# Column stage of an FFT mixer: the turn of U in three pieces, conversion slots moved, one product tile in PSUM

## The chip, the core and the metric

One core of a Trainium2 chip runs the whole program. The metric is device microseconds (us) of one execution; less is better. TensorE (PE) multiplies, VectorE (DVE), ScalarE (ACT) and GpSimd (POOL) work on tiles, and SyncE (SP) issues most DMAs. PEld is TensorE's weight load. All engines run their own queue strictly in order and wait for each other through semaphores.

## What is computed

```python
X = np.fft.rfft(x, axis=1)                       # x: 4 x 3136 x 256
y = np.fft.irfft(X * (filt_r + 1j * filt_i), n=3136, axis=1)
h = y.transpose(0, 2, 1) @ U @ V                 # U: 3136 x 32, V: 32 x 3136
u = y + h.transpose(0, 2, 1)
u = u + np.maximum(u @ w_ch1, 0.0) @ w_ch2       # 256 -> 1024 -> 256
xn = (u - mean) / np.sqrt(var + 1e-06) * g_ln    # over the 256 channels
out = u + np.maximum(xn @ w_ch1b, 0.0) @ w_ch2b
```

U, V and the weights arrive as 64-bit floats.

## The kernel before

The Fourier transform along the 3136 tokens is made by matmuls with tables, as 112 x 28. The program records all instructions in a fixed order; each engine's queue is that order, filtered by engine. It has three parts.

The first batch's transform runs alone. `rows()` turns 7 blocks of x by the row tables. Then `columns()` handles 14 pairs of 28 groups in 17 steps, j = 0 to 16; it is the stage of the change, and what follows names its parts as the text does later:
- **psz(j)**, L653: TensorE transposes pair 13 - j out of `big` into PSUM, ScalarE copies it to SBUF (z0). Odd steps take the PSUM pool ps_h (tag h, three banks), even ones ps_t (tag t, one bank).
- **ps2(j)**, L667: the pair of the step before is turned by the table e; then `filtered` multiplies it by the filter on VectorE: two products straight from PSUM (ya L635, xs L639) and two half sums (L641, L642), which GpSimd makes, or VectorE for the last pair (i = 0, step 14, with the products L638). ps2 takes banks of ps_h.
- **ps3(j)**, L678, from step 3 on: the pair that went through ps2 two steps earlier is multiplied back by the table d, whose last 32 columns hold the turned U, into two of the four output banks (`outer`, tags o0 to o3, in rotation). In the step after, ScalarE copies the result back into `big` (the spill) and VectorE adds the 32 columns of each bank to a sum (L622, L624), each behind the spill of the same bank.
- the **turn** of U, `u_half(1)` and then `u_half(0)`: a transposition on VectorE (L557), then one or two matmuls (pst, L562 and L563), the scaled copies uf by VectorE (L566) and the four copies uq by ScalarE (L219). From step 2 on, ScalarE copies a slice of uq into the table slot (`d<-uq`) of the pair that needs it two steps later.
- the filter loads for step j + 3 on SP's queue, and in step 1 two copies on GpSimd (L685) that fill the table slots.
- the **conversion slots**: `next(pr)` takes the conversion of weights and V from 64-bit to 32-bit numbers one slot further. A conversion begins every four slots: two reads by ScalarE (L976, L977), four operations on VectorE (L963, L965, L967, L969, one a slot), a product (L981) and a sum (L983) on GpSimd, three slots after the sum a copy by ScalarE (w1h, w2h, vh) and a slot later the low half on GpSimd (L1054, L1099). `COLSLOTS` says in which steps the slots lie: as often as it names a step, so many slots has it.

`UTURN` lists the steps in which the turn goes on by one piece; `UTURN.index(j) // 2` picks the half. In step 11 GpSimd issues the load of V (v_sb). Then `mixed` and `part` turn the columns back into tokens (psw, L725), and the first units (psu, L783, L785) begin.

The second part, most of the time, is the two-layer blocks, with the other three batches' transforms between them; the third is the rest of the blocks. `outer` gives them banks too.

Of the kernel before, what the change touches and what calls it, by code (L numbers as in the profile page):

```python
# [10 lines left out]
F32 = mybir.dt.float32  # L11
# [22 lines left out]
WARM, KEEP = 11, (0, 10, 5, 2, 2, 4, 1)  # L34
PUS, UTURN = ((), (0, 1), (2,), (3,), (4,), (5,), (6,)), (0, 1, 2, 3)
BACKL = 3
# [5 lines left out]
ROWSLOTS = (1, 2, 2, 3, 4, 5, 5, 5, 6)  # L42
COLSLOTS = (0, 0, 1, 1, 2, 2, 3, 3) + tuple(range(4, 12))
VSTEP = 11
# [139 lines left out]
def fft_mixer_kernel(ctx: ExitStack, tc: tile.TileContext, x, U, V, flt, w1, w2, gln, w1b, w2b,  # L184
# [261 lines left out]
    class First:  # L446
# [103 lines left out]
        def u_half(self, h):  # L550
# [13 lines left out]
            for lo, hi, wc in ((14, 28, w_sb[:, 0:1]),) if h else ((0, 1, w_sb[:, 1:2]), (1, 14, w_sb[:, 0:1])):  # L564
                src = ps[:, (lo - 14 * h) * R:(hi - 14 * h) * R].rearrange("p (g r) -> p g r", r=R)
                nc.vector.tensor_scalar(out=self.uf[:, lo:hi], in0=src, scalar1=wc, scalar2=None, op0=ALU.mult)  # L566
            for g in range(2):
                for k in range(2):
# [33 lines left out]
        def columns(self):  # L602
# [23 lines left out]
            def filtered(i, ps):  # L626
# [3 lines left out]
                else:  # L630
                    xs = fp.tile([P, 2, D], F32, tag="xs", name="xs", bufs=2)
                    ya = fp.tile([P, 2, D], F32, tag="ya", name="ya", bufs=4)
                src = ps.rearrange("p (a d) -> p a d", a=2)
                if i:
                    nc.vector.tensor_tensor(out=ya, in0=src, in1=f[:, 0:1].to_broadcast([P, 2, D]), op=ALU.mult)  # L635
                else:
                    for k, fr in enumerate((f[:, 0], self.nyquist)):
                        nc.vector.tensor_tensor(out=ya[:, k], in0=src[:, k], in1=fr, op=ALU.mult)  # L638
                nc.vector.tensor_tensor(out=xs, in0=src, in1=f[:, 1:2].to_broadcast([P, 2, D]), op=ALU.mult)  # L639
                eng = nc.gpsimd if i else nc.vector  # L640
                eng.tensor_tensor(out=ya[:, 0], in0=ya[:, 0], in1=xs[:, 1], op=ALU.subtract)  # L641
                eng.tensor_tensor(out=ya[:, 1], in0=ya[:, 1], in1=xs[:, 0], op=ALU.add)  # L642
                ys[i] = ya

            due = None
            for j in range(n + BACKL):
# [33 lines left out]
                if j in UTURN:  # L680
                    next(turns[UTURN.index(j) // 2], None)
                self.filters(j + AHEAD)
# [24 lines left out]
        def part(self, u, between=None):  # L707
# [4 lines left out]
            for dh in range(KT):  # L712
# [7 lines left out]
                if u < 2:  # L720
                    ps = outer("psw")
                else:
                    ps = (ps_t if dh else ps_h).tile([P, 512], F32, tag="t" if dh else "h", name="psw")
# [540 lines left out]
```

## Time and profile before

| | before |
|---|---|
| three timed runs | 1341.11, 1348.93, 1348.85 us; median 1348.85 |
| the profiled execution | 1340.96 us |
| its span in the profile | 1339.2 us |
| mean granted TensorE clock, share of full speed | 0.996 |
| TensorE busy | 1309.8 us (98%) |
| VectorE busy | 803.5 us (60%) |
| ScalarE busy | 428.9 us (32%) |
| GpSimd busy | 151.7 us (11%) |

Times in rows are us from the span's start. Busy shares are averages over stages with different limits, so the rows below are taken from the column stage. The row of a timeline gives start, duration (of several operations together, if it ends in a count over 1), engine, line, operation and its tiles; in brackets the engine's idle time ahead of it and what ended that.

### The profile page before, as it was taken

The page shows a single profiled execution, that of the slowest core. Times are in us where ns is not written, and L with a number is a line of the kernel's source. Part 1 is how long each engine was busy: PE and PEld are TensorE (multiplying, and loading weights), DVE is VectorE, ACT ScalarE, POOL GpSimd, SP SyncE. Part 2 cuts the span into 40 slices and gives each one's busy share as a digit, 9 for nine tenths or more (in the row PEclk, how much of TensorE's full clock was granted, in tenths as well). Part 3 has the DMA queues.
Part 4 walks back from the last instruction along what each step waited for, and adds up shares of the span by engine and source line. Part 5 has one row for each costly group of instructions (what it writes and reads, how often), then busy time and mean ns, then how long its engine had stood idle before and what let it go on. Part 6 is the DMA issues. An engine that isn't in the chain of part 4 may idle for free.

```text
span 1339.2 us, 22454 instructions
## 1 busy us (share of the span) xinstructions
PE 1309.8 (98%) x8606; PEld 1045.3 (78%) x8606; DVE 803.5 (60%) x1643; ACT 428.9 (32%) x857; POOL 151.7 (11%) x133
## 2 busy tenths in 40 slices
PE   8899999999999999999999999999999999999998
PEld 7578677777777877877777777878888888888887
DVE  5676985666656566575655666565455545555454
ACT  4456542333332233233322232232222222222222
POOL 1745530112000010010000010100000000000000
PEclk9899999999999999999999999999999999999999
DMA  9634447576565455434543554532112202210111
GB/s 236 173 99 140 114 109 220 150 226 173 148 178 148 120 150 145 127 99 114 165 144 96 140 159 113 144 90 65 32 34 65 65 16 67 65 40 9 47 49 40
DMA packets 166531, 151.15 MB, mean 113 GB/s; under 512 B 65912, under 2 KB 142568, under 8 KB 166424
## 3 DMA queue, kind: packets, MB, share of 16 engines
q1 hardware_dynamic: 166120, 148.25, 40.3%
q0 software_dynamic: 304, 1.47, 0.5%
q8 instruction: 68, 1.11, 0.3%
q14 instruction: 39, 0.32, 0.1%
HBM read 91.10 MB, written 47.54 MB: 104 GB/s over the span
## 4 chain that ended last, share of the span: by engine, by line
PE 85%; DVE 6%; DMA 4%; ACT 2%; SPq 2%; issue 1%; POOL 1%; DVEq 0%; POOLq 0%; ACTq 0%
PE psh L821 37%; PE pso L848 13%; PE pso L849 6%; PE pso L840 6%; PE pso L841 6%; PE pso L842 6%; PE psu L798 2%; DMA x<-x 2%; PE ps L301 1%; PE ps L375 1%; PE ps L341 1%; PE ps L678 1%; PE psu L803 1%; DVE hl L825 1%; PE ps L667 1%
## 5 line engine op out<-in xcount | busy, mean ns | idle before, releaser
L825 DVE SCALAR_TENSOR_TENSOR hl<-psh,hh 128x512 fp32r<-128x512 f32 (+1 forms) x400 | 271.5, 680 | 359.5 <-ACT hh L824 358.1
L824 ACT ACTIVATE hh<-psh 128x512 fp32r<-128x512 f32 (+1 forms) x400 | 234.8, 588 | 657.8 <-PE psh L821 657.6
L848 PE MATMUL pso<-wb,hh 128*128 128x512 f32 x784 | 285.0, 397 | 0.5 <-DVE x2t L888 0.3
L821 PE MATMUL psh<-ah,wb 128*128 128x512 f32 (+1 forms) x800 | 281.1, 393 | 0.6 <-DVE hl L825 0.6
L849 PE MATMUL pso<-wb,hl 128*128 128x256 f32 x784 | 219.7, 280 | 0.0
L821 PEld LDWEIGHTS psh<-ah,wb 128*128 128x128 f32 x800 | 150.1, 188 | 47.0 <-issue 6.0
L848 PEld LDWEIGHTS pso<-wb,hh 128*128 128x128 f32 x784 | 147.6, 188 | 35.4 <-DVE x L863 0.8
L821 PE MATMUL psh<-ah,w1h 128*128 128x512 f32 (+1 forms) x400 | 158.1, 395 | 0.0
L841 PE MATMUL pso<-hl,w2h 128*128 128x512 f32 (+1 forms) x400 | 154.4, 386 | 2.8 <-DVE hl L825 2.8
L840 PE MATMUL pso<-hh,w2h 128*128 128x512 f32 (+1 forms) x400 | 155.9, 390 | 0.4 <-DVE x2t L888 0.3
L821 PE MATMUL psh<-al,wb 128*128 128x512 f32 (+1 forms) x400 | 155.9, 390 | 0.0
L821 PE MATMUL psh<-al,w1h 128*128 128x512 f32 (+1 forms) x400 | 155.2, 388 | 0.0
L821 PE MATMUL psh<-ah,w1l 128*128 128x512 f32 (+1 forms) x400 | 154.3, 386 | 0.0
L842 PE MATMUL pso<-hh,w2l 128*128 128x512 f32 (+1 forms) x400 | 154.0, 385 | 0.0
L849 PEld LDWEIGHTS pso<-wb,hl 128*128 128x128 f32 x784 | 148.2, 189 | 7.5
L357 POOL TENSOR_TENSOR xs<-xs,ft 128x512 f32<-128x512 f32 x42 | 57.0, 1357 | 650.3 <-ACT hh L824 241.0
L821 PEld LDWEIGHTS psh<-ah,w1h 128*128 128x128 f32 x400 | 75.1, 188 | 22.5 <-issue 3.9
L888 DVE SCALAR_TENSOR_TENSOR x2t<-pso,ln,x2t 128x256 f32<-128x256 f32 x196 | 89.7, 480 | 3.6
L840 PEld LDWEIGHTS pso<-hh,w2h 128*128 128x128 f32 x400 | 75.1, 188 | 20.8 <-issue 5.6
L841 PEld LDWEIGHTS pso<-hl,w2h 128*128 128x128 f32 x400 | 75.2, 188 | 18.2 <-DVE hl L825 3.9
L821 PEld LDWEIGHTS psh<-ah,w1l 128*128 128x128 f32 x400 | 75.2, 188 | 15.9
L842 PEld LDWEIGHTS pso<-hh,w2l 128*128 128x128 f32 x400 | 75.1, 188 | 15.1
(150 smaller groups left out, 1341.7 us busy)
## 6 DMA issues: line engine op xcount, KB each, us to landing
ft<-flt SPq DMA_DIRECT2D x42, 512.0 KB
xd<-x SPq DMA_DIRECT2D x96, 128.0 KB
x2t<-xd SPq DMA_DIRECT2D x24, 512.0 KB
wt<-bd SPq DMA_DIRECT2D x48, 224.0 KB
out<-x2t SPq DMA_DIRECT2D x84, 128.0 KB
xs<-zc SPq DMA_DIRECT2D x168, 64.0 KB
xt<-x SPq DMA_DIRECT2D x84, 112.0 KB
zd<-ze SPq DMA_DIRECT2D x84, 112.0 KB
```

The costliest lines, as they stand in the source:

```text
L301: nc.tensor.matmul(pss[j][quarter(h), m * D:(m + 1) * D], ct[rows56(j), 2 * h + m], xs[h][rows56(j), m], start=True, stop=True)
L357: nc.gpsimd.tensor_tensor(out=xs, in0=xs, in1=fi[:, e], op=ALU.mult)
L798: nc.tensor.matmul(pss[h][c * HALF:(c + 1) * HALF, dh, h * spare + m:h * spare + half:UW], t[rows, m, d0:d0 + HALF], ic[rows, m, :], start ...
L821: nc.tensor.matmul(ps[:, :n], w[:, kt, fs], a[:, kt, :n], start=j == 0, stop=j == 3 * KT - 1)
L824: nc.scalar.activation(out=hh[:, :n], in_=ps[:, :n], func=AF.Relu)
L825: nc.vector.scalar_tensor_tensor(out=hl[:, :n], in0=ps[:, :n], scalar=0.0, in1=f32(hh[:, :n]), op0=ALU.max, op1=ALU.subtract)
L840: nc.tensor.matmul(o, wh[:, f, ds], hh[:, :n], start=f == 0, stop=False)
L841: nc.tensor.matmul(o, wh[:, f, ds], hl[:, :n], start=False, stop=False)
L842: nc.tensor.matmul(o, wl[:, f, ds], hh[:, :n], start=False, stop=f == FT - 1)
L848: nc.tensor.matmul(o, hh[:, cs], w, start=f == 0, stop=False, skip_group_check=True)
L849: nc.tensor.matmul(o[:, D:], hl[:, cs], w[:, :D], start=False, stop=f == FT - 1, skip_group_check=True)
L888: nc.vector.scalar_tensor_tensor(out=o, in0=acc[c][:, half * D:(half + 1) * D], scalar=rs[:, c:c + 1], in1=o, op0=ALU.mult, op1=ALU.add)
```

## The change

The turn of a half now has three pieces: the transposition, then the matmuls with uf, and, behind a new `yield`, the four uq copies. `UTURN` puts the pieces of the first half into steps 0, 1 and 2, those of the second into 3, 4 and 6 (before: two pieces each in steps 0 to 3). `COLSLOTS` gives one conversion slot each to steps 0 to 3, two to steps 4 to 7 and one to 8 to 11 (before: two in 0 to 3, one in 4 to 11); there are 16 both times. For the last pair the two products with the filter's real part go to a tile `yr` in PSUM (pool ps_t), from which the two sums are made. And the psw of part 0 takes banks of ps_h in place of output banks, so every output bank from there on is two further round the four.

```diff
-PUS, UTURN = ((), (0, 1), (2,), (3,), (4,), (5,), (6,)), (0, 1, 2, 3)
+PUS, UTURN = ((), (0, 1), (2,), (3,), (4,), (5,), (6,)), (0, 1, 2, 3, 4, 6)
...
-COLSLOTS = (0, 0, 1, 1, 2, 2, 3, 3) + tuple(range(4, 12))
+COLSLOTS = (0, 1, 2, 3) + tuple(j // 2 for j in range(8, 16)) + tuple(range(8, 12))
...
                 nc.vector.tensor_scalar(out=self.uf[:, lo:hi], in0=src, scalar1=wc, scalar2=None, op0=ALU.mult)
+            yield
             for g in range(2):
...
+                yr = ya
                 if i:
                     nc.vector.tensor_tensor(out=ya, in0=src, in1=f[:, 0:1].to_broadcast([P, 2, D]), op=ALU.mult)
                 else:
+                    yr = ps_t.tile([P, 512], F32, tag="t", name="yr").rearrange("p (a d) -> p a d", a=2)
                     for k, fr in enumerate((f[:, 0], self.nyquist)):
-                        nc.vector.tensor_tensor(out=ya[:, k], in0=src[:, k], in1=fr, op=ALU.mult)
+                        nc.vector.tensor_tensor(out=yr[:, k], in0=src[:, k], in1=fr, op=ALU.mult)
                 nc.vector.tensor_tensor(out=xs, in0=src, in1=f[:, 1:2].to_broadcast([P, 2, D]), op=ALU.mult)
                 eng = nc.gpsimd if i else nc.vector
-                eng.tensor_tensor(out=ya[:, 0], in0=ya[:, 0], in1=xs[:, 1], op=ALU.subtract)
-                eng.tensor_tensor(out=ya[:, 1], in0=ya[:, 1], in1=xs[:, 0], op=ALU.add)
+                eng.tensor_tensor(out=ya[:, 0], in0=yr[:, 0], in1=xs[:, 1], op=ALU.subtract)
+                eng.tensor_tensor(out=ya[:, 1], in0=yr[:, 1], in1=xs[:, 0], op=ALU.add)
...
                 if j in UTURN:
-                    next(turns[UTURN.index(j) // 2], None)
+                    next(turns[UTURN.index(j) // 3], None)
...
                 if u < 2:
-                    ps = outer("psw")
+                    ps = outer("psw") if u else inner("psw")
```

The line numbers below are those of each kernel's own source: from L567 on they are one higher after the change, from L634 on two, from L637 on three.

ScalarE's queue, steps 1 to 4, before (z_435 and z_479 are psz of steps 1 and 2, z_505 of step 3):

```order
L219 ACTIVATE z_435<-psz 112x512
L219 ACTIVATE uq<-uf 64x224 x4
L219 ACTIVATE w1h<-ct 128x512
L976 ACTIVATE cyh<-stg 128x392
L977 ACTIVATE cyl<-stg 128x392
L219 ACTIVATE z_479<-psz 112x512
L219 ACTIVATE d_187<-uq 128x2x32 x2
L219 ACTIVATE z_505<-psz 112x512
L219 ACTIVATE uq<-uf 64x224 x4
```

The same place after the change (z_434, z_463, z_488 and z_534 are steps 1 to 4):

```order
L219 ACTIVATE z_434<-psz 112x512
L219 ACTIVATE z_463<-psz 112x512
L219 ACTIVATE uq<-uf 64x224 x4
L219 ACTIVATE d_187<-uq 128x2x32 x2
L219 ACTIVATE z_488<-psz 112x512
L219 ACTIVATE d_187<-uq 128x2x32
L219 ACTIVATE w1h<-ct 128x512
L979 ACTIVATE cyh<-stg 128x392
L980 ACTIVATE cyl<-stg 128x392
L219 ACTIVATE z_534<-psz 112x512
```

Step 2's copy has moved ahead of the first uq copies and of the conversion, which now stands behind step 3's copy; the second uq copies have left the place altogether.

VectorE's queue, steps 4 and 5, before (ps_518 and ps_519 are ps3 of step 3, ps_578 and ps_579 of step 4):

```order
L622 COPY d_188<-ps_518 128x2x32
L622 COPY d_188<-ps_519 128x2x32
L635 TENSOR_TENSOR ya<-ps_567,f_301 128x512
L639 TENSOR_TENSOR xs<-ps_567,f_301 128x512
L963 TENSOR_SCALAR cyh<-cyh 128x512
L624 TENSOR_TENSOR d_188<-ps_578,d_188 128x2x32
L624 TENSOR_TENSOR d_188<-ps_579,d_188 128x2x32
```

The same place after the change (ps_501 and ps_502, ps_551 and ps_552):

```order
L623 COPY d_188<-ps_501 128x2x32
L623 COPY d_188<-ps_502 128x2x32
L637 TENSOR_TENSOR ya<-ps_540,f_301 128x512
L642 TENSOR_TENSOR xs<-ps_540,f_301 128x512
L566 TENSOR_SCALAR uf<-pst,w_sb 128x32
L566 TENSOR_SCALAR uf<-pst,w_sb 128x416
L966 TENSOR_SCALAR cyh<-cyh 128x392
L968 TENSOR_SCALAR ct<-cyh 128x392
L625 TENSOR_TENSOR d_188<-ps_551,d_188 128x2x32
L625 TENSOR_TENSOR d_188<-ps_552,d_188 128x2x32
```

Between step 4's products and the sums of its banks there are now four operations where there was one: uf of the second half and two of a conversion.

VectorE's queue, steps 14 and 15, after the change; before, the first two rows and the two sums have ya for yr, and the rest is the same:

```order
L641 TENSOR_TENSOR yr<-ps_949,f_788 128x256
L641 TENSOR_TENSOR yr<-ps_949,f_828 128x256
L642 TENSOR_TENSOR xs<-ps_949,f_788 128x512
L644 TENSOR_TENSOR ya<-yr,xs 128x256
L645 TENSOR_TENSOR ya<-yr,xs 128x256
L625 TENSOR_TENSOR d_188<-ps_962,d_188 128x2x32
L625 TENSOR_TENSOR d_188<-ps_963,d_188 128x2x32
```

No operation has moved here; what has changed is the memory in which the tile between them lies.

On TensorE only the second half's pst has moved, from behind step 3's ps3 to behind step 4's. On GpSimd the filter sums of steps 2 and 3 now stand ahead of a conversion's product (L981). On SP's queue one group of filter loads has moved ahead of two staging loads.

## Rows read from the trace of the kernel before

**Rows 1.** Windows: length; busy us by engine (instructions); granted clock; DMA share; GB/s.
```profile
38.00:48.40 10.40, 5.31 (x44) 3.38 (x44) 5.94 (x13) 6.77 (x19) 7.37 (x9) 1.00 0.75 205
48.40:55.50 7.10, 7.10 (x43) 5.20 (x43) 3.68 (x9) 1.23 (x4) 3.91 (x5) 0.52 0.85 207
55.50:78.00 22.50, 22.50 (x228) 15.71 (x228) 16.60 (x38) 13.19 (x39) 17.51 (x21) 1.00 0.54 142
...
140.00:180.00 40.00, 36.17 (x154) 25.79 (x154) 39.47 (x55) 18.72 (x35) 23.64 (x17) 1.00 0.42 108
```

**Rows 2.** Timeline of TensorE, step 10 and the start of step 11.
```profile
66.62 0.65 PE L653 MATMUL psz<-ident,big 128*112 128x128 f32 x4
67.20 1.08 PE L667 MATMUL ps<-z,e 112*64 112x256 f32 x8
68.21 1.26 PE L678 MATMUL ps<-d,ya 64*128 64x144 f32 x16
69.40 0.65 PE L653 MATMUL psz<-ident,big 128*112 128x128 f32 x4
```

**Rows 3.** Timeline of all engines, steps 2 and 3.
```profile
34.45 0.60 PE L653 MATMUL psz<-ident,big 128*112 128x128 f32 x4
...
35.93 1.59 ACT L219 ACTIVATE uq<-uf 64x224 f32<-64x224 f32 x4 [2.91 <-DVE uf L566]
...
37.13 1.00 POOL L685 COPY d<-d 128x336 f32<-128x336 f32 x2
...
38.98 0.57 ACT L219 ACTIVATE z<-psz 112x512 f32<-112x512 f32 x1
...
39.61 1.08 PE L667 MATMUL ps<-z,e 112*64 112x256 f32 x8 [2.96 <-ACT z L219]
```

**Rows 4.** Timeline of all engines, the second half's turn and step 4.
```profile
43.04 0.81 DVE L566 TENSOR_SCALAR uf<-pst,w_sb 128x32 f32<-128x32 f32 x2 [1.01 <-PE pst L563]
...
43.88 1.59 ACT L219 ACTIVATE uq<-uf 64x224 f32<-64x224 f32 x4 [3.55 <-DVE uf L566]
...
48.38 2.25 PE L678 MATMUL ps<-d,ya 64*128 64x144 f32 x14 [3.48 <-DVE d L622]
```

**Rows 5.** Timeline of all engines, steps 14 to 16.
```profile
78.88 0.76 DVE L638 TENSOR_TENSOR ya<-ps,f 128x256 f32<-128x256 f32 x2 [0.17 <-PE ps L667]
...
79.94 1.29 POOL L1054 TENSOR_TENSOR w2l<-ct,w2h 128x512 fp32r<-128x512 f32 x1
...
80.27 1.25 DVE L641 TENSOR_TENSOR ya<-ya,xs 128x256 f32<-128x256 f32 x1
...
81.44 1.48 DVE L642 TENSOR_TENSOR ya<-ya,xs 128x256 f32<-128x256 f32 x1
82.84 0.67 DVE L624 TENSOR_TENSOR d<-ps,d 128x64 f32<-128x64 f32 x4
...
83.11 1.38 PE L678 MATMUL ps<-d,ya 64*128 64x144 f32 x16 [2.06 <-DVE d L624]
```

**Rows 6.** Groups by line, first 160 us: total us, mean ns; idle time before.
```profile
L965 DVE TENSOR_SCALAR ct<-cyh 128x512 int32<-128x512 int32 (+1 forms) x15 | 15.5, 1032 | 0.3
...
L963 DVE TENSOR_SCALAR cyh<-cyh 128x512 f32<-128x512 f32 (+1 forms) x16 | 11.9, 742 | 0.0
L967 DVE SCALAR_TENSOR_TENSOR ct<-cyh,ct 128x512 int32<-128x512 int32 (+1 forms) x15 | 11.1, 741 | 0.0
...
L969 DVE TENSOR_SCALAR cyh<-ct 128x512 int32<-128x512 int32 (+1 forms) x15 | 6.6, 438 | 0.1
...
L635 DVE TENSOR_TENSOR hl<-ps,f 128x512 f32<-128x512 f32 x7 | 4.8, 690 | 1.3 <-DMA f<-flt 0.6 <-DMA stg<-w 0.5
```

**Rows 7.** Timeline: the issue of v_sb's load, and its first use.
```profile
75.61 0.81 POOL L1106 DMA_DIRECT2D v_sb<-vd x1
...
87.91 0.46 PE L785 MATMUL psu<-v_sb,tk 96*128 96x448 f32 x1
```

**Rows 8.** DMA issues by line, first 130 us: KB, median us from issue to landing.
```profile
v_sb<-vd POOLq DMA_DIRECT2D x1, 1176.0 KB, 9.2
```

## The prediction, made before the change was run

> **What bounds the kernel now.** I read the windows first. Nearly everywhere TensorE is busy the whole stretch at a granted clock of 1.00, and the change touches none of that work. The exceptions that concern it lie in the column stage, about 31 to 85 us. From 48.40 to 55.50 us the granted clock stands at 0.52, that is at the lower of its two levels, 1.2 GHz, while TensorE is busy without a gap; from 55.50 to 78.00 it is 1.00 and TensorE busy for all 22.50 us [rows 1]. The timeline of an undisturbed stretch gives the pace: step 10's transposes (psz) start at 66.62, its turning products (ps2) at 67.20, its back products (ps3) at 68.21, and step 11's psz at 69.40 [rows 2]. So a step costs 0.58 + 1.01 + 1.19 = 2.78 us when TensorE sets the pace, and at the lower clock about twice that.
>
> The timeline of steps 2 to 4 then shows three holes.
> - psz of step 2 has ended at 34.45 + 0.60 = 35.05, but ScalarE copies it out only at 38.98: ahead of that copy stand the four uq copies (35.93, 1.59 us, which began 2.91 us late because they wait for VectorE's uf) and a conversion slot. So ps2 of step 3 starts at 39.61 after 2.96 us of idle TensorE [rows 3].
> - In step 4 the same happens one link further. uf of the second half takes 0.81 us at 43.04, the uq copies 1.59 us from 43.88 after 3.55 us of waiting, then a conversion slot and the next psz copy, and only behind these the spill (big) whose bank VectorE must sum before ps3 of step 4 may go on: 48.38, after 3.48 us of idle TensorE [rows 4]. The clock falls right behind that hole and not behind the one of 2.96 us: it is 1.00 up to 48.40 [rows 1].
> - At the end, step 14's two sums take VectorE 1.25 and 1.48 us, though the products of the same size (L638) take 0.76 for two, that is about 0.4 each. The sum of step 15 waits behind them until 82.84, and the last ps3 starts at 83.11, 2.06 us after TensorE ran dry [rows 5].
>
> **The change, part by part.**
>
> *The turn in three pieces, one conversion slot in steps 0 to 3.* On ScalarE the first uq copies now stand behind psz(2)'s copy and the conversion two steps later. psz(2) can be copied out right when it ends, 35.05 + 0.6 = 35.6, so ps2(3) follows psz(3) with no hole, from about 36.6 to 37.6. uq then runs from about 35.7 to 37.3 and the two d copies to 37.7, before anyone needs them. What is last for ps3(3) now is GpSimd's copy of the tables, L685, which ends at 37.13 + 1.00 = 38.13 [rows 3]; the product ahead of it waits for VectorE about 0.2 us less, so I take 38.0. Before, ps3(3) started at 40.62, that is 39.61 + 1.01. Its first two matmuls go ahead of that wait, so it ends near 39.0. Behind it, from [rows 2]: psz(4) 39.0, ps2(4) 39.6, ps3(4) 40.6, the second half's pst 41.8. pst takes 0.8 us, the same as where it stood before. So psz(5) is at **42.6**.
>
> For step 4 to go that way, ScalarE must have psz(3) out by 39.6 (38.2, behind the d copies) and GpSimd step 2's sums by 40.6; with its conversion product gone from ahead of them these end near 39.8. The bank that step 4 waited for is now freed by uf of the first half, at 35.6. So neither the hole of 2.96 us nor the one of 3.48 us is left, and since the clock fell only behind the longer one, I count none of the slow stretch either.
>
> *Two conversion slots in steps 4 to 7.* This is the cost. A conversion has four VectorE operations with means of 0.74, 1.03, 0.74 and 0.44 us in the first 160 us [rows 6], together 2.95, so two slots cost 1.48 us a step. The step's own work on VectorE is two filter products of 0.69 [rows 6] and two sums (0.67 for four, so 0.34) [rows 5], 1.72 us. Together 3.20 us against TensorE's 2.78: VectorE becomes the bound and costs 0.42 x 4 = 1.7 us, and uf's 0.81 in step 4 [rows 4] adds to it: **2.5 us**. The bounds: nothing, if these operations sink into VectorE's waits (it was busy for 16.60 of 22.50 us with one slot [rows 1]); or, if all four cost the dearest's 1.03, 2.06 + 1.72 - 2.78 = 1.0 a step and 4.8 in all. GpSimd, busy 17.51 of those 22.50 us [rows 1], has the same load added and feeds ps3 two steps later; I put its delay into the same 2.5, since the two queues fill side by side.
>
> The clause of a rule stands beside this. The Trainium skill, "SBUF — State Buffer", section "Who interferes with whom", says that VectorE and GpSimd share a pair of ports as an exclusive lock: a VectorE operation of the two-port kind or with two SBUF inputs and a GpSimd operation that reads SBUF do not overlap, the later one waits for all of the other. By it the three single-source operations of a conversion would each risk a whole GpSimd operation once GpSimd is busy throughout. With 1.03 for these and 0.74 for the fourth, a step would cost 1.91 + 1.72 = 3.63, the four 3.4 and the stage 4.2 us, which is 1333.3 us instead of the sum below. The means lie lower, because in part of the cases nothing of GpSimd's is under way; rows decide.
>
> psz(10) then stands at 42.6 + 5 x 2.78 + 2.5 = 59.0, against 66.62: **7.6 us**, with 5.3 and 10.1 as its ends. From step 8 on the slots are as before, so the distance stays.
>
> *The last pair's products in PSUM.* The two sums now have one operand in PSUM. Beside GpSimd's work (L1054 at 79.94) VectorE's products from PSUM kept about 0.4 us while the sums from SBUF took 1.25 and 1.48 [rows 5]. With 0.42 each the second sum ends at about 81.1, step 15's two sums 0.3 later, and the last ps3 starts at 81.35 instead of 83.11: **1.75 us**. It can't be more than 2.06, since TensorE is busy until then, and it is nothing if writing and reading that tile in PSUM is no cheaper; no row shows VectorE writing PSUM.
>
> *At nothing:* the three operations of the turn's second half run later, but its slots are first copied in step 8, two steps behind; part 0's psw in the other pool, whose banks were read long before; the other rotation of the output banks, since each bank keeps one owner and the same distance to its next use. The filter loads on SP's queue move ahead of the staging loads by one group, and stagings behind them have two steps more until they are converted. *Late next:* v_sb is issued by GpSimd at 75.61, lands 9.2 us later, 84.8, and is read at 87.91 [rows 7, 8]. Only the gain at the tail eats this margin, 3.1 - 1.75 = 1.35 us.
>
> **Sum.** 7.6 + 1.75 = 9.35 us. The profiled execution took 1340.96 us, so 1331.6. Of the three timed runs one lies beside it (1341.11), two at 1348.93 and 1348.85, the median. What makes these 7.8 us isn't in the trace; if the run after has it, the same sum gives 1339.5.
>
> **Rivals.**
> 1. *As summed, at the upper of the two levels:* 1339.5. For it: two of three runs. Against it: the upper level may come from these very holes, one more fall of the clock behind a hole of 2.96 us, and they go.
> 2. *VectorE and ScalarE clog steps 4 to 9:* ScalarE's vh copies wait for GpSimd's sums, which wait behind step 4's and 6's filter sums, and the next psz copy stands behind them. Stage at its dear end and tail at nothing: 5.3 us, 1335.7.
> 3. *Absorbed later:* from 140 to 180 us VectorE is busy for 39.47 of 40 us and TensorE for only 36.17 [rows 1]. If that stretch were timed by something that doesn't move, the gain would be lost there: 1341. Against it: it is work in a fixed order that starts when the stage before it ends, and the amount of work is unchanged.
> 4. *Slower:* the doubled slots open a hole in step 5 as long as the one of 3.48 us, and the clock falls to 1.2 GHz there until the slots are single. At 5.56 us a step from 42.6, five steps end at 70.4, 3.8 later than before; with the tail's 1.75 the time is 1343.0. It decides from where five steps cost over 24 + 1.75 us, 5.15 each. Against it: the 2.5 us above are spread over four steps, so that no single hole is near 3.48 us.
>
> **Chances.** As summed 0.52; rival 1 0.24; rival 2 0.12; rival 3 0.06; rival 4 0.06. Likeliest is 1331.6; by its own bounds (7.6 from 5.3 to 10.1, tail from 0 to 2.06) it lies between 1328.8 and 1335.7. For 8 in 10 the range must take in rivals 1 and 2: 1328 to 1341. Over 1% means below 1335.4 or above 1362.3 against the median of 1348.85; about so much can be told from no change here. The likeliest case and a little of rival 2 are below 1335.4: 0.50. Within 1%: 0.48. Slower by over 1% has no case with a price that large: 0.02.
>
> **What would show it.** Right: no hole over 2 us on TensorE from 36 to 80 us, granted clock 1.00 throughout, ScalarE's uq copies behind psz(2)'s copy, psz(10) between 56.5 and 61.5, step 14's two sums under 0.5 us each, and all later stages earlier by one distance. Wrong: a clock of 0.5 anywhere in the stage; ScalarE waiting for GpSimd ahead of a vh copy by more than 2 us; sums above 1 us; a wait of psu for v_sb; or a distance that shrinks between 90 and 180 us.

## The result and the profile after

The changed kernel took 1332.71 us, the median of six runs (1329.34 to 1337.05). The kernel before, run beside it, took 1344.11 us (median of six, 1341.08 to 1348.93). The ratio is 0.991 with a 95% interval of 0.9881 to 0.994, so the gain is 0.6% to 1.2%, 11.4 us by the medians. The profiled execution took 1329.34 us, against 1340.96 before.

| | before | after |
|---|---|---|
| profiled execution | 1340.96 us | 1329.34 us |
| its span | 1339.2 us | 1327.6 us |
| mean granted TensorE clock | 0.996 | 0.999 |
| TensorE busy | 1309.8 us | 1305.5 us |
| VectorE busy | 803.5 us | 800.6 us |
| GpSimd busy | 151.7 us | 151.4 us |

The windows of after come first (length; busy us by engine, PE, PEld, DVE, ACT, POOL, with their instructions; granted clock; DMA share; GB/s). The first two answer to those of [rows 1]:

```profile
38.00:48.40 10.40, 9.56 (x89) 6.65 (x88) 8.71 (x20) 6.27 (x18) 8.92 (x10) 1.00 0.72 192
48.40:55.50 7.10, 6.03 (x61) 4.09 (x61) 4.88 (x9) 4.18 (x13) 6.61 (x7) 1.00 0.63 169
55.50:70.00 14.50, 13.88 (x140) 9.51 (x138) 12.29 (x28) 8.46 (x27) 12.45 (x15) 1.00 0.74 208
...
200.00:220.00 20.00, 18.85 (x171) 14.68 (x170) 10.73 (x29) 5.49 (x12) 0.00 (x0) 1.00 0.73 239
```

From 38.00 to 48.40 TensorE ran 89 instructions where it ran 44. The stretch at 0.52 is gone.

The timeline of TensorE shows where each step begins (start, duration, line, tiles; in brackets the idle time ahead and what ended it). Each psz row is the start of a step, up to step 13:

```profile
28.69 1.06 PE L656 MATMUL psz<-ident,big 128*112 128x128 f32 x8 [0.78 <-DVE big L537]
...
36.17 1.26 PE L681 MATMUL ps<-d,hl 64*128 64x144 f32 x16 [0.81 <-ACT d L219]
...
41.17 0.60 PE L656 MATMUL psz<-ident,big 128*112 128x128 f32 x4
...
44.07 1.23 PE L681 MATMUL ps<-d,hl 64*128 64x144 f32 x14 [0.84 <-DVE d L625]
...
55.29 1.08 PE L670 MATMUL ps<-z,e 112*64 112x256 f32 x8 [1.07 <-ACT z L219]
...
57.49 0.65 PE L656 MATMUL psz<-ident,big 128*112 128x128 f32 x4
...
63.05 1.02 PE L681 MATMUL ps<-d,hl 64*128 64x144 f32 x12 [0.62 <-POOL hl L645]
...
66.79 0.65 PE L656 MATMUL psz<-ident,big 128*112 128x128 f32 x4
...
73.17 1.38 PE L681 MATMUL ps<-d,ya 64*128 64x144 f32 x16 [0.30 <-DVE d L625]
...
75.12 0.67 PE L728 MATMUL psw<-ident,big 128*112 128x128 f32 x4 [0.57 <-DVE d L625]
```

The holes of 2.96, 3.48 and 2.06 us of [rows 3 to 5] are gone. What stands in this stage instead are five short ones: 0.81, 0.84, 1.07, 0.62 and 0.30. Step 5 begins at 41.17, step 10 at 57.49, step 13 at 66.79.

To compare traces I use three lengths that do not depend on when the stage begins: the **stage**, from the first psz to the first psw; its **steps**, from the first psz to step 13's; and its **tail**, the rest.

| us | before | after | difference |
|---|---|---|---|
| start of the first psz | 30.93 | 28.69 | -2.24 |
| steps | 44.04 | 38.10 | -5.94 |
| tail | 10.10 | 8.33 | -1.77 |
| first psw to the end of the span | 1254.13 | 1252.48 | -1.65 |
| span | 1339.2 | 1327.6 | -11.6 |

So 7.7 of the 11.6 us lie in the stage that the change touches. The 2.24 us ahead of it are no work of the change: the stage begins behind the loads of x, and in the other traces of before its first psz starts elsewhere (29.66 in one). The 1.65 us behind it can't be put down to the change either: in a second trace of after (e11_after_again) the same length is 1256.54, longer than before's. In the first profile of before the granted clock falls in this part, and in the profile of after it doesn't:

```profile
200.00:220.00 20.00, 18.34 (x155) 14.94 (x152) 11.43 (x27) 4.58 (x9) 0.00 (x0) 0.91 0.73 224
```

That row is before, in the same window as the last of after above: 0.91 against 1.00. The fall begins behind a hole of TensorE, in the next batch's transform:

```profile
207.52 1.21 PE L301 MATMUL ps<-xt,ct 56*64 56x256 f32 x16 [1.66 <-DVE x2t L888]
```

At the same place after waits 1.44 us (until 197.39), without a fall.

### The profile page after: what moved, and what is told of

Its sections match the earlier page's. It is cut to its first block, busy times and chain, and to the rows that moved or that the text cites. A ratio compares the mean times of both kernels' runs of the same rounds, so it can differ in the third digit from the quotient of the medians.

```text
span 1327.6 us, 22451 instructions
## 1 busy us (share of the span) xinstructions
PE 1305.5 (98%) x8606; PEld 1042.0 (78%) x8606; DVE 800.6 (60%) x1643; ACT 428.7 (32%) x857; POOL 151.4 (11%) x133
## 4 chain that ended last, share of the span: by engine, by line
PE 84%; DVE 5%; DMA 5%; POOL 2%; SPq 1%; ACT 1%; issue 1%; DVEq 0%; POOLq 0%; ACTq 0%
PE psh L824 37%; PE pso L851 13%; PE pso L852 6%; PE pso L843 6%; PE pso L844 6%; PE pso L845 6%; PE psu L801 2%; PE ps L301 1%; PE ps L375 1%; PE ps L341 1%; DMA zd<-ze 1%; PE psu L806 1%; DVE hl L828 1%; DMA stg<-v 1%; PE pt L381 1%
```

## The experiments

**The theory.** The gain is in the stage, from two causes. Turn and slots together take the two holes and the slow clock out of the steps, and since neither is enough alone, each alone leaves one hole. The PSUM tile takes the wait of the last pair's sums for GpSimd out of the tail. **The rival** for the columns: one of the two edits does it all, and the other is idle. **For the tail**: the sums got cheaper because of PSUM itself or of the banks, not because GpSimd was in their way. **For the rest**: the medians differ by more than the stage, so part of it lies elsewhere (banks, later stages). In the diffs, - is before unless said otherwise, and ... stands for lines that are left out.

### Turn and slots without the tail (e1_columns)

```diff
-PUS, UTURN = (...), (0, 1, 2, 3)
+PUS, UTURN = (...), (0, 1, 2, 3, 4, 6)
...
-COLSLOTS = (0, 0, 1, 1, 2, 2, 3, 3) + tuple(range(4, 12))
+COLSLOTS = (0, 1, 2, 3) + tuple(j // 2 for j in range(8, 16)) + tuple(range(8, 12))
...
+            yield
...
-                    next(turns[UTURN.index(j) // 2], None)
+                    next(turns[UTURN.index(j) // 3], None)
```

> Turn in three pieces and moved slots alone; the last pair's product stays in SBUF and psw keeps its banks. Measured as the stage from the first psz to the first psw (before 54.1 us, after 46.4). My theory, that columns and tail add up: the holes of 2.96 and 3.48 us are gone, the granted clock is 1.00 throughout, the stage takes 48.2 us and the last ps3 waits about 2.0 us again. Rival, that the tail's gain hangs on the earlier columns (or the reverse): the stage differs from 48.2 by over 0.5 us. Time by my theory 6 us below the kernel before, 0.995 or 0.996 of it.

Measured: 1337.24 us against 1344.34, ratio 0.9947 (0.9925 to 0.9969). The steps took 37.94 us, the tail 11.14, longer than before's 10.10. Windows of this kernel, columns as above:

```profile
30.00:74.00 44.00, 39.26 (x374) 26.66 (x374) 36.16 (x73) 25.41 (x73) 38.91 (x43) 1.00 0.77 199
74.00:81.50 7.50, 6.49 (x37) 6.02 (x37) 2.92 (x13) 2.65 (x6) 0.00 (x0) 0.54 0.00 0
```

The columns' part is as in the full change, with the clock at 1.00 throughout. But the tail's hole of 2.06 us is back, and here the clock fell to the lower level behind it, which it did not in the first trace of before. The stage, 49.08 us, missed my 48.2 by 0.88, more than the 0.5 that I had allowed. That isn't the columns: from step 13 to the last ps3 it took as long as in before (8.15 and 8.14 us), and the 1.04 us more in the tail come behind the hole, with the slow clock.

### The product tile in PSUM alone (e2_tail)

```diff
+                yr = ya
...
+                    yr = ps_t.tile([P, 512], F32, tag="t", name="yr").rearrange("p (a d) -> p a d", a=2)
-                        nc.vector.tensor_tensor(out=ya[:, k], in0=src[:, k], in1=fr, op=ALU.mult)
+                        nc.vector.tensor_tensor(out=yr[:, k], in0=src[:, k], in1=fr, op=ALU.mult)
...
-                eng.tensor_tensor(out=ya[:, 0], in0=ya[:, 0], in1=xs[:, 1], op=ALU.subtract)
-                eng.tensor_tensor(out=ya[:, 1], in0=ya[:, 1], in1=xs[:, 0], op=ALU.add)
+                eng.tensor_tensor(out=ya[:, 0], in0=yr[:, 0], in1=xs[:, 1], op=ALU.subtract)
+                eng.tensor_tensor(out=ya[:, 1], in0=yr[:, 1], in1=xs[:, 0], op=ALU.add)
```

> The product tile in PSUM alone. My theory: the last two sums take about 0.42 us each, the last ps3 waits 0.3 us for its bank, the stage takes 52.4 us, 1.75 less, and nothing else changes; holes of 3 and 3.5 us and the low clock stay. Rival, that VectorE's write to PSUM costs as much as it saves: the two products take 1.5 us or more each and the stage stays at 54.1. In the whole time 1.75 us can hardly be told from nothing.

Measured: 1340.67 us, ratio 0.9978 (0.9961 to 0.9994). Steps 44.05, tail 8.33. VectorE's timeline:

```profile
76.13 0.90 DVE L640 TENSOR_TENSOR yr<-ps,f 128x256 f32<-128x256 f32 x2 [0.17 <-PE ps L669]
...
77.65 0.42 DVE L643 TENSOR_TENSOR ya<-yr,xs 128x256 f32<-128x256 f32 x1
78.00 0.41 DVE L644 TENSOR_TENSOR ya<-yr,xs 128x256 f32<-128x256 f32 x1
```

Two sums of 0.42 and 0.41 us where 1.25 and 1.48 stood [rows 5]; writing the two products to PSUM costs 0.90 instead of 0.76. The tail's gain is its own and does not depend on the columns. Both holes of the columns remain, and here the clock fell behind both, the shorter too:

```profile
37.00:41.50 4.50, 4.50 (x28) 3.03 (x27) 1.74 (x3) 0.57 (x2) 4.50 (x6) 0.62 0.91 260
47.00:51.50 4.50, 4.27 (x26) 3.08 (x26) 2.09 (x7) 1.37 (x6) 2.90 (x4) 0.62 1.00 211
```

Still the steps are as long as in the first trace of before, which had the clock at 1.00 behind its first hole. That is because two falls of different length cancel out. The second hole ends here at 47.23:

```profile
47.23 2.05 PE L680 MATMUL ps<-d,ya 64*128 64x144 f32 x14 [3.49 <-DVE d L622]
```

That is 19.06 us after the first psz (28.17); in before it was 17.45 (30.93 to 48.38). So the fall behind the first hole cost 1.61 us. From the end of the second hole to step 13 it took 24.99 us (to 72.22), and in before 26.59 (to 74.97). So the fall behind the second hole cost 1.60 us less here, with 4.50 us at 0.62 against 7.10 at 0.52 [rows 1].

### The turn alone (e3_turn) and the slots alone (e4_slots)

The first takes the UTURN, `yield` and `// 3` lines of e1_columns, the second only its COLSLOTS line.

> The turn in three pieces alone, slots still two in steps 0 to 3. My theory: both parts are needed for the whole, since a conversion's ScalarE operations (about 1.7 us) still stand ahead of a psz copy in the first steps; holes of about 1.2 us are left there, under 3 us, the clock stays at 1.00, steps 4 to 7 go at 2.78 us each, and the stage takes about 49.5 us without the tail's part. Rival, that the slots alone made the holes: the hole of about 3 us and the low clock are still there and the stage takes 53 us or more.

> The moved slots alone, the turn still in two pieces in steps 0 to 3. My theory: uq still stands ahead of a psz copy, so a hole of about 2 us stays at step 3 and one of about 2 us at step 4, both too short for the clock to fall, and steps 4 to 7 cost about 2.5 us more; the stage takes about 50.7 us. Rival, that the turn alone made the holes: one of 3 us or more stays, the clock falls behind it, and the stage takes 54 us or more.

Measured, the turn: 1341.73 us, ratio 0.9975 (0.9958 to 0.9992), steps 40.11, stage 50.21. The slots: 1341.87, ratio 0.9984 (0.9964 to 1.0005), steps 42.82, stage 52.92. Against 44.04 the turn gives 3.9 us of the steps, the slots 1.2, both 6.1 (e1_columns). Part of these sums is the clock: the fall in before was worth 3.2 us (e8_warm below), those in these two runs by their windows below about 1.5 each (an estimate, 3.50 x 0.44 and 3.40 x 0.44). By the same estimate, without the clock the turn would give about 2.3, the slots nothing and both 2.9.

With the turn alone a hole of 2.89 us stands at 44.48. ScalarE's timeline shows why:

```profile
41.81 0.53 ACT L219 ACTIVATE vh<-ct 128x392 fp32r<-128x392 f32 x1 [3.63 <-POOL ct L984]
...
43.34 0.58 ACT L219 ACTIVATE z<-psz 112x512 f32<-112x512 f32 x1
```

With two slots in each of steps 0 to 3 a copy of vh comes up in step 4 and waits 3.63 us for GpSimd's sum. The psz copy and the spill stand behind it, as they stood behind uq before. This is the wait that rival 2 named, and here it is the early slots that make it (with the late ones such a copy waits 2.88 us in the changed kernel, see below). With the slots alone the old chain of [rows 4] is still there:

```profile
41.44 1.58 ACT L219 ACTIVATE uq<-uf 64x224 f32<-64x224 f32 x4 [3.42 <-DVE uf L566]
```

uq waits 3.42 us for uf, and TensorE's holes are 1.24 us in step 3 and 3.37 in step 4. So neither edit does it alone: each removes the work that would stall the same queue at the same place, and one of them alone leaves the other's. The queue shows this, more than the signs that I had set: in both runs the hole of about 3 us and the slow clock of the rival came true, and only the stage stayed under the rival's 53 and 54 us.

I missed sizes in both: stages of 49.5 and 50.7 us were expected. The slots alone kept a hole of 3.37 us, with the slow clock behind it (its windows):

```profile
45.80:49.20 3.40, 3.38 (x22) 2.59 (x24) 2.36 (x5) 0.43 (x2) 2.00 (x3) 0.56 0.94 262
```

The turn alone has its hole of 2.89 where I had expected short ones, and the same behind it:

```profile
44.50:48.00 3.50, 3.50 (x14) 1.95 (x16) 2.67 (x6) 0.87 (x4) 2.05 (x3) 0.56 0.89 201
```


### The change without the banks (e5_outer_psw)

From the changed kernel:

```diff
-                    ps = outer("psw") if u else inner("psw")
+                    ps = outer("psw")
```

> The changed kernel with part 0's psw in the output banks as before, so the main part has the old bank rotation. My theory: costs and brings nothing; stage 46.4 us and the distance between the first psw and the end as in the changed kernel, 1252.5 us, within the spread of runs. Rival, that the other banks brought the 1.6 us by which the changed kernel's main part was shorter: that distance goes back to 1254.1 us, and the whole is 1.6 us slower.

Measured: 1332.13 us (1331.64 to 1334.76) against 1342.64, ratio 0.9918 (0.9902 to 0.9935); steps 37.27, tail 8.33. The other banks bring nothing that can be told. The sign that I had set for it doesn't decide: from the first psw to the end this profiled execution took 1257.98 us, more than 1252.5 and 1254.1, but it was the slowest of the four, and in it the clock fell twice behind psw. Over all the traces that length lies between 1252.48 and 1258.42.

### The kernel before, once more (e6_before_again), and the changed one (e11_after_again)

No edit in either.

> The kernel before once more, for its profile. My theory: the first psz, 30.9 us in the one profile and 28.7 in the changed kernel's, moves by one to three us from run to run with the loads of x, and so do 1 to 2 us of the main part; the stage from first psz to first psw stays at 54.1 +- 0.5. Rival, that the earlier start belongs to the change: the first psz stays at 30.9 +- 0.3.

Measured: 1346.26 us, span 1344.5. Stage 56.42, of it steps 45.61 and tail 10.81. Windows behind its three holes (3.06, 3.49 and 2.06 us):

```profile
38.30:43.00 4.70, 4.66 (x28) 3.42 (x29) 1.93 (x3) 0.77 (x3) 4.70 (x6) 0.64 0.87 221
48.70:57.00 8.30, 8.24 (x52) 5.73 (x54) 3.75 (x9) 2.03 (x8) 4.91 (x6) 0.59 0.89 210
83.40:91.00 7.60, 7.01 (x41) 6.57 (x41) 3.17 (x11) 2.64 (x6) 0.00 (x0) 0.55 0.00 1
```

In this execution the clock fell behind all three; in the first trace it fell behind the middle one alone. I had expected a stage of 54.1 +- 0.5. It is 2.28 us longer: 1.65 up to the end of the second hole, 0.71 in the tail, and 0.08 less between them.

> The changed kernel once more, beside the last on the same chip. Theory, that the holes were what let the clock fall: no stretch below 1.00 between 28 and 100 us in this trace either, and its times spread less than those of the kernel before in the same session. Rival, that the absence in the first trace was chance: the clock falls behind one of the holes of 0.6 to 1.1 us.

Measured: 1332.57 us (1332.12 to 1333.41) against 1342.59, ratio 0.9922 (0.9898 to 0.9947). Stage 45.68 and steps 37.34, of which 28.06 to step 10 (29.38 to 57.44). The hole of 0.81 us in step 3 isn't there. Its windows:

```profile
28.00:100.00 72.00, 67.26 (x564) 51.01 (x564) 55.44 (x117) 42.81 (x110) 47.13 (x50) 1.00 0.59 150
300.00:340.00 40.00, 38.37 (x229) 28.26 (x229) 24.58 (x52) 13.11 (x27) 8.00 (x6) 0.96 0.57 151
```

No fall in the stage, but one far behind it, and it too begins behind a hole of TensorE:

```profile
318.56 0.50 PE L824 MATMUL psh<-ah,wb 128*128 128x512 f32 x1 [1.63 <-DVE hl L828]
```

Its four runs lie within 1.3 us, the eleven of before beside them within 8.4.

### TensorE kept busy in the long hole (e8_warm)

```diff
+WARM4 = 14
...
+                    for _ in range(WARM4 if j == 4 else 0):
+                        nc.tensor.matmul(pvs[0][:, 0, :P], ones, ones, start=True, stop=True)
```

These products are extra work whose results nobody reads; they stand in step 4 ahead of the matmuls that wait.

> The kernel before with 14 products of ones (3.4 us at the higher clock) put ahead of step 4's ps3, into a bank that ps3 overwrites, so that TensorE is busy in the hole of 3.48 us. Theory, that the low clock behind that hole is part of the gain: the granted clock stays at 1.00 from 48 to 56 us, steps 4 and 5 cost 3 us less, and the stage takes about 51 us. Rival, that the slow steps have another cause: the clock falls all the same, or it stays and the steps are as long as before, 54.1.

Measured: 1337.44 us. The timeline and the windows:

```profile
45.00 3.39 PE L676 MATMUL ps<-ones 128*128 128x128 f32 x28
...
49.02 1.22 PE L681 MATMUL ps<-d,ya 64*128 64x144 f32 x14 [0.19 <-DVE d L623]
```

```profile
38.60:43.00 4.40, 4.40 (x27) 3.08 (x28) 1.89 (x3) 0.73 (x3) 4.37 (x6) 0.61 0.88 237
45.00:80.00 35.00, 33.34 (x338) 24.58 (x336) 25.62 (x56) 20.18 (x60) 26.51 (x30) 1.00 0.72 173
```

The wait is still there, only filled, and behind it the clock stays at 1.00. From step 5 to step 13 (psz at 50.18 and 72.44) the eight steps now take 22.26 us, which is 8 x 2.78; before they took 24.40 (50.57 to 74.97). The rest of step 4's ps3 takes 1.16 us (49.02 to 50.18) where it took 2.19 (48.38 to 50.57). Together 3.2 us: the price of that slow stretch alone, measured with the hole left in place. I expected a stage of 51 us and got 52.63, because here the clock fell behind the hole of 2.98 us at 38.60, ahead of the products: from the first psz to step 4's ps3 it took 19.10 us (29.92 to 49.02), 1.65 more than before's 17.45.

### GpSimd kept out of the way of the last sums (e7_quiet, e9_quiet)

The first leaves the conversion slots of the main part's first step out:

```diff
-                next(pr, None)
+                if idx:
+                    next(pr, None)
```

> The kernel before with the two conversion slots of the main part's first step left to the next, so that GpSimd has nothing to do while VectorE makes the last pair's two sums from SBUF. Theory, that two SBUF operands wait for GpSimd's: the sums fall from 1.25 and 1.48 to about 0.42 each and the last ps3 waits 0.3 us, without any tile in PSUM; stage 52.4. Rival, that an operand in SBUF is slower as such: they stay above 1 us and the stage at 54.1.

Measured: 1342.51 us. It didn't do what it was made for: GpSimd had work left on its queue and ran it at the same time, and the sums from SBUF took 1.26 and 1.48 us again. It still shows how they collide:

```profile
78.53 1.30 POOL L1054 TENSOR_TENSOR w2l<-ct,w2h 128x512 fp32r<-128x512 f32 x1
```

```profile
78.85 1.26 DVE L641 TENSOR_TENSOR ya<-ya,xs 128x256 f32<-128x256 f32 x1
80.03 1.48 DVE L642 TENSOR_TENSOR ya<-ya,xs 128x256 f32<-128x256 f32 x1
```

GpSimd's operation ends at 79.83 and the first sum at 80.11, 0.28 later; in the first trace it was 0.29 (79.94 + 1.29 = 81.23, and 81.52) [rows 5].

The second makes GpSimd wait: a copy of one column that needs the last sum stands ahead of the next conversion on its queue.

```diff
+                if i == 0:
+                    nc.gpsimd.tensor_copy(xs[:, 0, 0:1], ya[:, 1, 0:1])
```

> The kernel before with one small copy (128x1) on GpSimd behind the last pair's two sums, so that GpSimd must wait for them and has nothing under way while VectorE makes them from SBUF. Theory, that the sums waited for GpSimd's operations: they fall from 1.25 and 1.48 to about 0.4 each, the last ps3 waits 0.3 us in place of 2.06, and from the last psz to the first psw it takes 8.3 us in place of 10.1, with no tile in PSUM. Rival, that an operand in SBUF is slow as such: the sums stay above 1 us and the hole at 2.06.

Measured: 1339.72 us. Stage 52.27, tail 8.20, with no hole of 2.06. VectorE and GpSimd:

```profile
78.68 0.42 DVE L641 TENSOR_TENSOR ya<-ya,xs 128x256 f32<-128x256 f32 x1
79.02 0.42 DVE L642 TENSOR_TENSOR ya<-ya,xs 128x256 f32<-128x256 f32 x1
```

```profile
79.57 0.19 POOL L645 COPY xs<-ya 128x1 f32<-128x1 f32 x1 [1.17 <-DVE d L624]
```

With everything in SBUF and GpSimd idle the sums take 0.42 each. So PSUM is not cheaper in itself: the 0.83 and 1.06 us were the wait for GpSimd's operations, and the tile in PSUM is one way round it.

### The double slots spread out (e10_spread, e12_early_ic)

From the changed kernel. Its own cost is the four double steps in a row, so here only steps 5 and 7 are double, and the last slots move to steps 12 and 13:

```diff
-COLSLOTS = (0, 1, 2, 3) + tuple(j // 2 for j in range(8, 16)) + tuple(range(8, 12))
+COLSLOTS = (0, 1, 2, 3, 4, 5, 5, 6, 7, 7) + tuple(range(8, 14))
```

> The changed kernel with slots in steps 0 to 4, two in 5 and in 7, one each in 6 and 8 to 13 (16 as before). My theory, that two slots a step are what is left as cost: the holes of 0.84 us in step 5, 1.07 in step 9 and 0.62 in step 11 shrink to under 1 us together, from first to last psz it takes about 36 us in place of 38.1, and the whole is 1 to 2 us under the changed kernel, at the edge of what can be told. Rival, that GpSimd or the load of V is the limit, which now waits for a later write: a new wait of 1 to 3 us of GpSimd in step 11 or of psu for v_sb, and no gain.

Measured: 1332.72 us (1329.88 to 1335.07) against 1342.59, ratio 0.9924 (0.9905 to 0.9944). The steps took 34.70 us, 3.4 less than in after and 2.6 less than in its second trace, and still nothing came of it:

```profile
76.30 1.12 PE L786 MATMUL psu<-ic,wt 112*128 112x112 f32 x8 [2.24 <-DMA ic<-c_inv]
```

```profile
66.81 0.39 SPq L960 DMA_DIRECT2D stg<-w  x1
67.25 13.82 SPq L748 DMA_DIRECT2D ic<-c_inv  x4
```

SP's queue issued a staging load only at 66.81, as that waits for ScalarE's later reads, and the tables for psu stood behind it: issued at 67.25, against 64.40 in after. psu waited 2.24 us, and from the first psz to the first psu it took 47.92 us, against 48.46 in after and 47.71 in its second trace. Neither my theory nor the rival had named this load. So the tables for the first two units were moved ahead (from e10_spread):

```diff
+                if j == 8:
+                    wt.update((u, new_unit(u)) for u in range(2))
...
-            if u < DIRECT:
+            if u < DIRECT and u not in wt:
```

> The spread slots again, with the tables ic of the first two units loaded in step 8, ahead of the last staging load, whose wait for ScalarE held them back before. Theory, that this wait alone gave the spread's gain back: psu no longer waits for ic, from the first psz to the first psu it takes 45.5 us (48.5 in the changed kernel, 47.9 with the spread alone), and the whole is about 2 us under the changed kernel, 1330 to 1331 us. Rival, that something behind is late anyway (v_sb's load, or the conversions' operations that wait behind the same stage in the main part): a new wait of about 2 us before 120 us, and no gain.

Measured: 1331.64 us (1331.19 to 1332.98, six runs) against 1344.06, ratio 0.9907 (0.9885 to 0.9928). From the first psz to psu now 46.40 us, 1.3 less than the shorter of after's two, and no wait for the tables:

```profile
76.69 1.04 PE L788 MATMUL psu<-ic,wt 112*128 112x112 f32 x8
```

```profile
55.84 0.94 SPq L750 DMA_DIRECT2D ic<-c_inv  x2
```

I had expected 45.5. The 0.9 more are short waits ahead of psu: 0.35 and 0.34 us for GpSimd's sums and 0.58 and 0.49 for VectorE, where after has 0.30 and 0.57.

It is the lowest median of all the kernels that were run, about 1 us below the changed kernel's two (1332.71 and 1332.57). The intervals of the ratios overlap widely, so the difference in time is not shown; the shorter stage is.

## Why the prediction was right, and where not

**The bound and the columns.** Predicted was 7.6 us for step 10's start. Reckoned from the first psz it came 6.89 us earlier in the profile after (35.69 to 28.80) and 7.63 in the second trace (28.06). The steps of it:
- uq behind psz(2)'s copy and no hole in steps 2 to 4: as forecast. What was missed is the 0.81 us at 36.17. VectorE's first product stood waiting for its filter load, and the d copies came late behind it:

```profile
32.23 0.69 DVE L637 TENSOR_TENSOR hl<-ps,f 128x512 f32<-128x512 f32 x1 [1.72 <-DMA f<-flt]
```

In that execution the load came later than the stage could use it. e1_columns shows the same, a wait of 1.52 us for the load and a hole of 0.57. In e5_outer_psw, the second trace of after and e10_spread the hole isn't there, though e10_spread began as early (28.38). From the first psz to step 5 the forecast was 11.67 us; it was 12.48 = 11.67 + 0.81.
- the double slots: 2.5 us was forecast to step 10. From step 5 to step 10 it took 16.32 us, that is 5 x 2.78 + 2.42. The size was right, and that is in part luck: VectorE did not become the bound, for steps 6, 7 and 8 took 2.78 us each. The cost did not come as an even 0.42 a step, as reckoned, but mostly in two holes, both behind what the forecast named: 0.84 in step 5, where a sum stands behind uf and two conversions, of which the second took 1.31 us and ended 0.22 behind GpSimd's operation (42.11 to 43.57), and 1.07 in step 9, where ScalarE's vh waited 2.88 us for GpSimd ahead of the psz copy:

```profile
42.48 1.31 DVE L968 TENSOR_SCALAR ct<-cyh 128x392 int32<-128x392 int32 x1
43.71 0.34 DVE L625 TENSOR_TENSOR d<-ps,d 128x64 f32<-128x64 f32 x2
```

```profile
53.10 0.53 ACT L219 ACTIVATE vh<-ct 128x392 fp32r<-128x392 f32 x1 [2.88 <-POOL ct L986]
...
54.66 0.57 ACT L219 ACTIVATE z<-psz 112x512 f32<-112x512 f32 x1
```

That vh wait is over the 2 us that the prediction set as a sign against itself. The sign was there and the price was 1.07 us, within the 2.5: rival 2's mechanism is real, at less than its price.
- "From step 8 on the slots are as before, so the distance stays": wrong. Steps 10 to 12 took 9.30 us (57.49 to 66.79) where before they took 8.35 (66.62 to 74.97), 0.95 more. The one hole there, 0.62 us at 63.05, waits for a GpSimd sum that took 1.18 us; the rest of the 0.95 shows no row of its own. The same stands in the other four traces with these slots (9.28 to 9.31, e4_slots among them), and 8.35 in all seven with the old ones. So GpSimd's backlog from the double slots reached past step 8. The whole cost of the slots to step 13 is 25.62 - 8 x 2.78 = 3.38 us. This is the term that was mis-sized, by 0.9.

Beside the rule that the prediction weighed: by the Trainium skill, "SBUF — State Buffer", section "Who interferes with whom", the slots would have cost 4.2 us, an estimate with prices from rows; by the rows alone 2.5. Measured were 2.42 to step 10 and 3.38 to step 13, the whole between the two. The estimate counted only the three single-source operations; the fourth reads two tiles in SBUF (L967, ct from cyh and ct, [rows 6]), which the rule covers as well.

**The tail.** Forecast 1.75 us, measured 1.77. The rows:

```profile
70.70 0.90 DVE L641 TENSOR_TENSOR yr<-ps,f 128x256 f32<-128x256 f32 x2 [0.17 <-PE ps L670]
...
72.22 0.42 DVE L644 TENSOR_TENSOR ya<-yr,xs 128x256 f32<-128x256 f32 x1
72.56 0.41 DVE L645 TENSOR_TENSOR ya<-yr,xs 128x256 f32<-128x256 f32 x1
```

GpSimd's operation ran across them (71.75 to 73.05) and did not hold them up:

```profile
71.75 1.30 POOL L1057 TENSOR_TENSOR w2l<-ct,w2h 128x512 fp32r<-128x512 f32 x1
```

The reason given was that the sums waited for GpSimd; e9_quiet shows it directly, since without GpSimd's work beside them they take 0.42 from SBUF too. The same section of the Trainium skill says that a VectorE operation with two SBUF inputs and a GpSimd operation that reads SBUF block each other, the later one waiting for all of the other, and that one with at most one SBUF input, outside the two-port kinds, doesn't contend. This agrees with the sums that ended 0.28 us behind GpSimd's operation in e7_quiet, and with the 0.42 of the sums with one input in PSUM.

**Nothing late next.** v_sb was issued at 67.11, landed 7.7 us later at 74.8 and its first reader started at 77.97 without a wait. Its issue moved up along with the steps. The banks at nothing: the times of e5_outer_psw show no difference.

**The clock.** "The clock fell only behind the longer one" was read off one execution, and as a rule it was wrong. Over the traces of kernels that have these holes, the clock fell behind that of 3 us in step 3 in five of six, behind that of 2.9 to 3.5 us in step 4 in seven of seven, and behind that of 2.06 in the tail in four of seven. Behind the 2.24 us of e10_spread, ahead of psu, it didn't fall, nor behind any hole up to 1.24. It did not harm the forecast, since the change removes all three holes.

But it explains a part of what the prediction left open. The 7.8 us between the three runs shown were not two levels: 27 runs of before, in the comparison with e1_columns, lie spread from 1339.70 to 1349.57, with mean granted clocks from 0.996 down to 0.988. The span of e6_before_again is 5.3 us longer than that of the first trace: 2.28 of this lie in the stage and 1.83 from psw to psu, behind the tail's hole, 2.46 lie further on, and its first psz came 1.27 earlier. The first trace, at 1340.96 us, was one of the shorter executions. Against the second trace of before, the stage of after's second trace is 10.7 us shorter, and the medians differ by 10 to 11.4. So rival 1 asked the right question, and the answer is in part the one that it gave against itself: more falls behind these holes, which are gone. Only in part, since the ten runs of the changed kernel spread over 7.7 us too (1329.34 to 1337.05).

Rival 3 fell: from the first psw to the hole near 200 us, that is over the stretch that it named, it took 120.79 us in before and 120.83 and 120.77 in the two traces of after. Rival 4 fell: no hole in step 5 over 0.84 us, and no fall.

**What made the sum come out.** 1331.6 against 1329.34 for the profiled execution and 1332.71 for the median. In the profiled one 7.71 us came from the stage instead of 9.35, and 3.9 from outside of it that nothing in the sum stood for. In the runs as a whole the stage's share is probably larger: the execution from which the sum was made had a mean clock of 0.996, the highest of the 27 runs' 0.988 to 0.996, but no trace of a run at the median shows where the others lost theirs. That the forecast stands so near to both is partly luck, since these two balance. Its 0.50 for a gain over 1% was reckoned against the median of three runs, 1348.85; against 1344.11, the median of six, the gain is 0.9%.

**What stays open.** What decides in one execution whether the clock falls behind a hole of 1.5 to 3 us. The falls in the main part, where the change alters nothing but banks, are of the same kind. The 14 traces have 15 of them, and each begins behind a hole of TensorE of 1.52 to 3.11 us, 11 times ahead of a product of a later batch's transform (L301). Other holes of these lengths passed without a fall. The one near 200 us lasted between 1.31 and 3.11 us from execution to execution; no run here tells what sets its length.

## What to carry to other kernels

In queues that run strictly in order, a stall belongs to whatever stands ahead in the queue, and taking one such thing away uncovers the next: here two edits that gave 3.9 and 1.2 us of the steps alone gave 6.1 together, the slow clock included. When a stage gets shorter, look at the loads whose issue waits for an engine's reads; in e10_spread 2.6 to 3.4 us were won in the steps, and most of it was lost again to a table that stood behind one staging load. And read a clock that fell in one execution as a chance, not as a fact of the kernel: a second trace of the unchanged kernel costs little, and here it changed the stage by 2.28 us.

## What the runs showed of the hardware

- Behind holes of TensorE between 2.06 and 3.5 us in the column stage the granted clock fell to the lower level in 16 of 20 cases, and the same hole in the same kernel did so in one execution and not in the next. In the main part it fell behind 15 holes of 1.52 to 3.11 us and not behind others of these lengths; behind holes up to 1.44 us it fell in no trace.
- A fall in the column stage stands in windows of 3.4 to 8.3 us at a mean clock of 0.52 to 0.64. It cost 3.2 us behind step 4's hole in before (26.59 us to step 13, against 23.42 in e8_warm), 1.57 behind the same hole in e2_tail (24.99), and 1.6 behind step 3's (19.06 us in e2_tail against 17.45).
- Filling the hole with products that nobody reads kept the clock at 1.00 behind it in the one execution of e8_warm; left empty, a hole of 2.89 to 3.49 us in that step brought a fall in all seven traces.
- VectorE wrote two 128x256 fp32 products to PSUM in 0.90 us, against 0.76 to SBUF. A sum of that size took 0.42 us with one operand in PSUM and 0.42 with both in SBUF, as long as GpSimd was idle; with both in SBUF and GpSimd at work 1.25 to 1.48.
